# Chunk 1's three rounds u = v + N u in a DeltaNet + SwiGLU kernel: units of odd bp on exchanged halves

## The chip, the cores and the metric

One core of one Trainium2 chip runs the whole program in one launch. The metric is device time in microseconds. Three runs of the kernel before gave 695.55, 698.75 and 694.11 us; their median is 695.55. Everything is float32.

## The reference

Two blocks, one after the other. The first is a gated delta rule: for each of 4 batches and 8 heads a 48x48 state is read and updated token by token over 768 tokens. Its output is laid side by side by head (8 x 48 = 384 columns) for 3072 tokens and goes through a SwiGLU feed-forward block.

```python
B, H, S, D = 4, 8, 768, 48
k_n = k / (norm(k) + 1e-06)
for t in range(S):
    kt, vt, bt = k_n[:, :, t], v[:, :, t], beta[:, :, t, None]
    y[:, :, t] = einsum('bhd,bhde->bhe', q[:, :, t], state)
    v_old = einsum('bhde,bhd->bhe', state, kt)
    state = state + bt[..., None] * einsum('bhd,bhe->bhde', kt, vt - v_old)
x = y.transpose(0, 2, 1, 3).reshape(3072, 384)
g, val = x @ w_gate, x @ w_val            # 384 x 1536 each
out = (g / (1 + exp(-g)) * val) @ w_out   # 1536 x 384
```

## The kernel before

The 768 tokens are cut into 12 chunks of 64. Inside a chunk the recurrence is a triangular system over 64 tokens, one for each of the 32 pairs of batch and head. A pair is called a unit, and has four indices: b and bp (batch = 2 b + bp), j and par (head = 2 j + par). A unit's 64 tokens lie in one half of the 128 partitions, rows 0 to 63 or 64 to 127; `half_of(x)` is that half. TensorE is used as four quadrants of 64x64: the half that a unit's operands lie in is the quadrant's rows, the half of PSUM's partitions that it writes to is its columns.

For chunks 2 and later the inverse of the triangular matrix is made whole, by VectorE or GpSimd. For chunks 0 and 1, which stand at the head of the program, only the four diagonal blocks of 16 tokens are inverted (`zt`), and the rest is done by rounds. A matrix N is formed for each unit (L734, from `l_sb` and `zt`, copied from PSUM to `n_sb` by ScalarE at L739). Then v0 is the product of `zt` and the scaled v (L950), copied to SBUF at L962, and three times u = v0 + N u is taken: 32 products of a 64x64 N and a 64x48 u on TensorE (L970), then one sum on VectorE over 128x768 (L1353, in the helper `plus`). Four blocks of 16 are why three rounds are enough.

`advance(c)` is a generator that does this for chunk c. For c = 1 it yields after the v0 products and after each of the first two rounds, and the driver puts half of a feed-forward product (L1282: three matmuls of 128x128 by 256) behind each yield, with one or two conversions of weight pieces. So the order of work on each engine is written out in the program; there is no other scheduler. Round, half product, round, half product, round, half product, then the state's update (L1018, added at L1027) and the chunk's output (L1006, copied to `y` at L1063 and L1065), then transposes (L1079, copied at L1085).

In chunk 1 `every()` walks the units in the order bp, j, then (par, b) = (0,0), (1,1), (0,1), (1,0). L950 reads rows of half b ^ par and writes half b; the N products read half b ^ par and write half b too. After that a unit's N, v0 and u all lie in half b, and the rounds (`by_par` with flip = 0) read half b and write half b. One bank holds par 0, the other par 1.

At the same time the weights come in. Each is loaded as words in pieces, put together by ScalarE (L272, L278) and VectorE (L289, L297, L309), and each piece's place is loaded again by SyncE when its conversion is done (L260). SyncE also loads q, k and v of later chunks (L140, L186). ScalarE makes silu (L1291), VectorE the product with the second factor (L1293). L1309 is the output product of the first two chunks; from chunk 2 on the feed-forward block takes other forms (L1186, L1392).

Of the kernel before, what the change touches and what calls it, by code (L numbers as in the profile page):

```python
# [8 lines left out]
FP32 = mybir.dt.float32  # L9
# [4 lines left out]
C = 64  # L14
# [6 lines left out]
def kernel(  # L21
# [25 lines left out]
    nc = tc.nc  # L47

    B, H, S, D = q.shape
    NCH = S // C  # L50
    NJ = H // 2
    NB = B // 2
# [5 lines left out]
    HH = NB * H  # L58
# [4 lines left out]
    work = ctx.enter_context(tc.tile_pool(name="work", bufs=2))  # L63
# [10 lines left out]
    def ps_pair(name, tag):  # L74

        return pairs_of_banks[tag]
# [21 lines left out]
    qpad = [const.tile([128, NB, H, DP], FP32, name=f"qpad{i}") for i in range(QB)]  # L98
# [224 lines left out]
    for b in range(2):  # L323
        rows = mask_q[64 * b : 64 * b + 64]
        nc.gpsimd.affine_select(
            out=rows,
            in_=rows,
# [23 lines left out]
    def half_of(x):  # L351
        return slice(64 * x, 64 * x + 64)
# [4 lines left out]
    def every():  # L357
        for bp in range(NB):
            for j in range(NJ):
                for n, (par, b) in enumerate(ORDER):  # L360
                    yield bp, j, par, b, bp == 0 and j == 0
# [104 lines left out]
    def scale_v(c, engine=nc.vector):  # L466
        scaled.add(c)
        if c > 1:
            spent.append(1.4)
        r = vin[c].rearrange("p par bp j d -> p (par bp j) d")  # L470
        n = n_t[c // 2][:, c % 2, :, None].to_broadcast([128, HH, D])
        engine.tensor_tensor(out=r, in0=r, in1=n, op=ALU.mult)

    def banks(name, tag):

        if type(tag) is int:
            return [ps_ffn([128, 512], name, tag + i) for i in range(2)]
        p = ps_pair(name, tag)
        return [p[:, 0], p[:, 1]]
# [87 lines left out]
    WAIT, MORE = "wait", "more"  # L567
# [40 lines left out]
    first_of, l_sb, n_sb = {}, {}, {}  # L608
# [118 lines left out]
    def n_products(c, p_n, pars):  # L727

        zt = ztp[0][:, c]
        p_v = [p.rearrange("p (bp j i) -> p bp j i", bp=NB, j=NJ) for p in p_n]  # L730
        for bp, j, par, b, _ in every():
            if par in pars:
                rows, h = half_of(b ^ par), HH // 2 * par + NJ * bp + j
                nc.tensor.matmul(  # L734
                    p_v[par][half_of(b), bp, j], l_sb[c][rows, h], zt[rows, h]
                )

    def n_copy(c, p_n, par):
        nc.scalar.copy(  # L739
            n_sb[c][:, par].rearrange("p bp j i -> p (bp j i)"), p_n[par]  # L740
        )

    def new_nt(c, flat):
        n_sb[c] = flat.rearrange("p (par bp j i) -> p par bp j i", bp=NB, par=2, j=NJ)

    def recur(p, m=D):
        p = p[:, :, 0 : NB * NJ * m]
        return p.rearrange("p x (bp j d) -> p x bp j d", bp=NB, j=NJ)
# [150 lines left out]
    def advance(c):  # L899

        kn = kn_of(c)
        zt = ztp[c // 2 % ZB][:, c % 2]
        zt = zt.rearrange("p (par bp j) i -> p par bp j i", par=2, bp=NB)
# [3 lines left out]
        if c > 0:  # L907
            p_y = recur(ps_pair("p_y", "py"))
            p_r = recur(ps_pair("p_r", "px"))
            for bp, j, par, b, first in every():  # L910
# [4 lines left out]
                    start=first,  # L915
                    stop=True,
                    skip_group_check=True,
                )
            for bp, j, par, b, first in every():
# [4 lines left out]
                    start=first,  # L924
                    stop=False,
                    skip_group_check=True,
# [4 lines left out]
        def new_u(name):  # L931
            return work.tile([128, 2, NB, NJ, D], FP32, name=name, tag="r", bufs=2)

        def single(bank):
            return [
                p[:, 0 : NB * NJ * D].rearrange("p (bp j d) -> p bp j d", bp=NB, j=NJ)
                for p in banks("p_u", bank)
            ]

        p_u = recur(ps_pair("p_u", "px"))  # L940
        p_u_of = [p_u[:, 0], p_u[:, 1]]

        v0 = new_u("uu" if c > 1 else "v0")
        if c == 0:
            p_n = banks("p_n", "py")
            n_products(c, p_n, (0, 1))
            for par in range(2):
                n_copy(c, p_n, par)
        for bp, j, par, b, first in every():
            nc.tensor.matmul(  # L950
                p_u_of[par][half_of(b), bp, j],
                zt[half_of(b ^ par), par, bp, j],
                r[half_of(b ^ par), par, bp, j],
                start=first,
                stop=True,
                skip_group_check=True,
            )
        if c == 0:
            nc.vector.tensor_copy(v0[:, 0], p_u[:, 0])
            nc.scalar.copy(v0[:, 1], p_u[:, 1])  # L960
        else:
            nc.scalar.copy(v0, p_u)  # L962
        uu = v0

        def by_par(p, stationary, moving, flip, start):
            for par in range(2):
                for bp in range(NB):
                    for j in range(NJ):
                        for b in range(2):
                            nc.tensor.matmul(  # L970
                                p[par][half_of(b ^ par * flip), bp, j],
                                stationary[half_of(b), par, bp, j],
                                moving[half_of(b), par, bp, j],
                                start=start and bp + j == 0,
                                stop=True,
                                skip_group_check=True,
                            )
                yield par

        if c < 2:  # L980
            yield MORE
            uu = new_u("uu")
            p_n = single(2) if c == 0 else p_u_of
            for n in range(3):
                for par in by_par(p_n, n_sb[c], uu if n else v0, 0, True):
                    if c == 0:
                        plus(uu[:, par], v0[:, par], p_n[par])
                        if n + par < 3:
                            yield MORE
                if c > 0:  # L990
                    plus(uu, v0, p_u)
                    if n < 2:
                        yield MORE
        if c + 2 < NCH:
            if c < 2:
# [45 lines left out]
        if c == 0:  # L1041
            third = single(2)[0]
            for par in range(2):
                for bp in range(NB):
                    p = third if par and bp else p_y[par]
                    for j in range(NJ):
                        for b in range(2):
# [4 lines left out]
                                start=j == 0 and (bp == 0 or par == 1),  # L1052
                                stop=True,
                                skip_group_check=True,
# [20 lines left out]
        for bp in range(NB):  # L1075
            for t in range(KT):
                at = slice(t * 128, (t + 1) * 128)
                p = p_f[bp][:, t] if c == 0 else p_f[:, t, bp]
# [26 lines left out]
    def units(t):  # L1105
        return t.rearrange("p (u n) -> p u n", u=4)
# [74 lines left out]
    p_x, p_w, p_y, p_v = (units(bank) for bank in ffn_banks)  # L1181
# [170 lines left out]
    def plus(out, a, b):  # L1352
        nc.vector.tensor_tensor(out=out, in0=a, in1=b, op=ALU.add)  # L1353
# [235 lines left out]
    def point(c):  # L1589

        mine = c < NCH and steps("advance", c) < 4 and may_advance(c)
        if mine and steps("advance", c) > 0:
            step("advance", advance, c)
        elif not prep_step(c - 1) and mine:
            step("advance", advance, c)

    def finish(c):

        if c < NCH:
            while not may_advance(c):  # L1600
                fill_some(1000)
                prep_step(c - 1)
            while steps("advance", c) < 4:
                step("advance", advance, c)
# [27 lines left out]
    with tc.manual_schedule(  # L1632
# [63 lines left out]
        zb_1 = work.tile([128, R, R], FP32, name="zb", bufs=1)  # L1696
# [11 lines left out]
        converts_first(2)  # L1708
        p_n = banks("p_n", "px")
        n_products(1, p_n, (0,))  # L1710
        step("advance", advance, 0)
        converts_first(4)
        n_products(1, p_n, (1,))
        converts_first(1, 3)
        converts_first(5)
        scale_v(1)
        for par in range(2):
            n_copy(1, p_n, par)

        def chain(at):  # L1720

# [70 lines left out]
```

## Time and profile before

| | |
|---|---|
| median of three runs | 695.55 us (694.11 to 698.75) |
| the profiled execution | 697.58 us, of which the span from first to last instruction is 695.9 us |
| instructions | 25446 |
| mean granted TensorE clock | 0.996 of full |
| TensorE busy, 46.0 to 58.1 us | 10.63 of 12.10 us |
| TensorE busy, 75.2 to 140 us | 64.75 of 64.80 us |
| HBM | 53.58 MB read, 7.08 MB written |

The profile is of one execution. Times in it are counted from the start of its span. PE is TensorE's matmuls, PEld its weight loads (which overlap), DVE is VectorE, ACT ScalarE, POOL GpSimd, SP SyncE. In a timeline a row has the start, the length from the first start to the last end, engine, line, operation, what it writes and reads, partitions and elements, and how many records it merges; a bracket at the end is the idle time of the engine before it and what ended it. A 64x64 or 128x128 float32 matmul is two matmul records and two weight loads. The length of a TensorE row has the last matmul's latency in it, so that the next row starts before it is over: the time that a row takes is read from start to start. "issue" is a wait for nothing that the profile shows.

### The profile page before, as it was taken

Reading aid. Unit: us, or ns where it says so; the run is one execution under the profiler, and the core shown is the slowest. Engines: PE = TensorE matmul, PEld = TensorE weight load, DVE = VectorE, ACT = ScalarE, POOL = GpSimd, SP = SyncE. Lnnn points to the kernel's source line nnn. Section 1 sums busy time; section 2 is a strip of 40 time slices with the busy share of each in tenths; the row PEclk is TensorE's granted clock in tenths of the full one; section 3 lists DMA queues with packets and bytes.
Section 4 is the critical chain, followed back from the end, with each engine's and each line's share of the span. In section 5 each row is a group of like instructions: output and inputs, shape, how many; then the busy total and the mean of one; then the engine's idle time right before and its main releaser. Section 6 shows DMA issues by size and latency. Waiting matters only on the chain.

```text
span 695.9 us, 25446 instructions
## 1 busy us (share of the span) xinstructions
PE 680.5 (98%) x11272; PEld 634.9 (91%) x11272; DVE 410.3 (59%) x857; ACT 258.7 (37%) x548; POOL 192.3 (28%) x310
## 2 busy tenths in 40 slices
PE   7799999999999999999999999999999999999997
PEld 4597888756999999999999999999999999999997
DVE  6876789798666745557446547465565345333342
ACT  4754776204543533343333245233143242142230
POOL 5010031105893037830037830328800000000000
PEclk9999999999999999999999999999999999999999
DMA  9566925006561532464333373233263221221210
GB/s 133 141 167 171 288 63 167 1 23 156 140 121 25 103 92 40 92 118 92 78 86 70 67 138 73 56 83 73 64 122 70 55 63 46 56 62 46 69 47 23
DMA packets 143854, 62.29 MB, mean 90 GB/s; under 512 B 122977, under 2 KB 126049, under 8 KB 143745
## 3 DMA queue, kind: packets, MB, share of 16 engines
q1 hardware_dynamic: 141536, 60.19, 37.5%
q8 instruction: 88, 1.44, 0.9%
q10 hardware_dynamic: 2080, 0.39, 0.4%
q14 instruction: 22, 0.17, 0.1%
q0 software_dynamic: 128, 0.10, 0.1%
HBM read 53.58 MB, written 7.08 MB: 87 GB/s over the span
## 4 chain that ended last, share of the span: by engine, by line
PE 93%; SPq 2%; DMA 2%; ACT 1%; issue 1%; DVE 1%; POOL 0%; DVEq 0%; ACTq 0%
PE ffn L1186 43%; PE ffn L1392 20%; PE ffn L1282 9%; PE ffn L1309 4%; PE p_px L950 2%; PE p_px L911 2%; PE p_py L920 2%; PE p_px L1018 1%; PE p_py L1006 1%; PE p_py L521 1%; SPq L140 1%; PE p_px L521 1%; PE ffn L970 1%; DMA h_f<-in_moe_w_gate_dram 1%; PE p_py L1079 1%
## 5 line engine op out<-in xcount | busy, mean ns | idle before, releaser
L1186 PE MATMUL ffn<-x_ffn,wg_sb 128*128 128x128 f32 x840 | 128.2, 275 | 0.0
L1186 PE MATMUL ffn<-x_ffn,wv_sb 128*128 128x128 f32 x840 | 128.1, 275 | 0.0
L1186 PEld LDWEIGHTS ffn<-x_ffn,wg_sb 128*128 128x128 f32 x840 | 111.1, 192 | 0.1
L1186 PEld LDWEIGHTS ffn<-x_ffn,wv_sb 128*128 128x128 f32 x840 | 110.7, 192 | 0.0
L1221 DVE TENSOR_TENSOR h_f<-sil,ffn 128x256 f32<-128x256 f32 x120 | 50.0, 418 | 78.5 <-ACT sil L1216 76.9
L1216 ACT ACTIVATE sil<-ffn 128x256 f32<-128x256 f32 x120 | 46.0, 383 | 132.6 <-PE ffn L1186 130.9
L1392 PE MATMUL ffn<-wo_sb,h_f 128*128 128x192 f32 x480 | 83.4, 327 | 0.0
L813 POOL TENSOR_TENSOR n_b<-mb,half 128x32 f32<-128x32 f32 x5 | 30.0, 6008 | 182.2 <-DVE mb L563 182.2
L1392 PEld LDWEIGHTS ffn<-wo_sb,h_f 128*128 128x128 f32 x480 | 78.1, 190 | 0.4
L1353 DVE TENSOR_TENSOR ffn<-ffn,p_sb 128x512 f32<-128x512 f32 x58 | 40.5, 699 | 63.7 <-ACT ffn L1242 62.4
L599 POOL TENSOR_TENSOR zb<-zb,tmp 128x31 f32<-128x31 f32 (+15 forms) x124 | 71.5, 576 | 9.7
L593 POOL TENSOR_TENSOR tmp<-zb,mb 128x31 f32<-128x31 f32 (+15 forms) x124 | 67.0, 541 | 16.0 <-DVE mb L580 6.6
L1186 PE MATMUL ffn<-x_t,h_f 128*128 128x128 f32 x480 | 61.1, 280 | 0.2 <-ACT ffn L1199 0.2
L1186 PEld LDWEIGHTS ffn<-x_t,h_f 128*128 128x128 f32 x480 | 56.2, 191 | 1.4 <-ACT ffn L1199 0.4
L1353 DVE TENSOR_TENSOR o_sb<-o_sb,ffn 128x192 f32<-128x192 f32 x49 | 17.2, 352 | 61.9 <-PE ffn L1392 60.7
L1199 ACT COPY ffn<-ffn 128x512 f32<-128x512 f32 x30 | 17.1, 571 | 63.9 <-PE ffn L1186 57.5
L1392 PE MATMUL ffn<-last_k,h_f 128*128 128x192 f32 x200 | 35.9, 327 | 0.0
L1350 DVE TENSOR_TENSOR h_f<-h_f,h_f 128x256 f32<-128x256 f32 x60 | 30.2, 512 | 9.2 <-PE ffn L1392 8.2
L1282 PE MATMUL ffn<-x_ffn,wg_sb 128*128 128x256 f32 x144 | 34.3, 384 | 0.0
L1282 PE MATMUL ffn<-x_ffn,wv_sb 128*128 128x256 f32 x144 | 33.8, 382 | 0.0
L1392 PEld LDWEIGHTS ffn<-last_k,h_f 128*128 128x128 f32 x200 | 32.9, 190 | 0.0
L1282 PEld LDWEIGHTS ffn<-x_ffn,wv_sb 128*128 128x128 f32 x144 | 27.0, 190 | 3.7
(300 smaller groups left out, 1095.6 us busy)
## 6 DMA issues: line engine op xcount, KB each, us to landing
h_f<-w_s SPq DMA_DIRECT2D x60, 256.0 KB, 2.9
p_sb<-w_s SPq DMA_DIRECT2D x27, 256.0 KB, 2.8
vin<-in_v_dram SPq DMA_DIRECT2D x48, 96.0 KB, 3.4
out_dram<-o_sb SPq DMA_DIRECT2D x48, 96.0 KB, 2.2
kn<-in_k_dram SPq DMA_DIRECT2D x20, 192.0 KB, 4.6
zt<-in_moe_w_out_dram SPq DMA_DIRECT2D x6, 384.0 KB, 3.3
qpad<-in_q_dram SPq DMA_DIRECT2D x36, 64.0 KB, 3.1
w_s<-h_f SPq DMA_DIRECT2D x7, 256.0 KB, 4.2
```

The lines of the kernel that those rows point to most:

```text
L593: engine.tensor_tensor(out=t_v, in0=zb[:, 0 : j + 1, j : j + 1].to_broadcast([128, j + 1, m]), in1=mb[:, j : j + 1, j + 1 : R].to_broadcas ...
L599: engine.tensor_tensor(out=zb[:, 0 : j + 1, j + 1 : R], in0=zb[:, 0 : j + 1, j + 1 : R], in1=t_v, op=ALU.add,)
L813: nc.gpsimd.tensor_tensor(out=n, in0=mb.rearrange("p j i -> p (j i)")[:, 0 : R * R : R + 1], in1=half, op=ALU.pow,)
L1186: nc.tensor.matmul(p[:, u], w(u), moving, start=start and u == 0, stop=True, skip_group_check=True,)
L1199: nc.scalar.copy(p_y, p_x)
L1216: nc.scalar.activation(sil[:, n].rearrange("p (i n) -> p i n", i=2), p[:, 0:2], ACTF.Silu)
L1221: nc.vector.tensor_tensor(out=h_of(c, f, j), in0=sil[:, n].rearrange("p (i n) -> p i n", i=2), in1=p[:, 2:4], op=ALU.mult,)
L1282: nc.tensor.matmul(ps[name][:, i], w_sb[:, t, (f + i) * 128 : (f + i + 1) * 128], xts[c][:, t], start=(t == 0 and i == 0), stop=(t == KT - 1),
L1309: nc.tensor.matmul(p_o, hs[c, f - f % 2][:, f % 2, bp * 128 : (bp + 1) * 128], wo_sb[:, f], start=(f == 0), stop=(f == FT - 1),)
L1350: nc.vector.tensor_tensor(out=out, in0=a, in1=b, op=ALU.subtract)
L1353: nc.vector.tensor_tensor(out=out, in0=a, in1=b, op=ALU.add)
L1392: nc.tensor.matmul(p[x, part], a(f - f % 2)[:, f % 2], b(f), start=not begun and f == 0, stop=f == FH - 1, skip_group_check=True,)
```

## The change

The change is in chunk 1 alone, and in its rounds. Units with bp = 1 change halves before each round and come back in the next, so that of four units one after the other (bp = 0 and 1, b = 0 and 1) each uses another quadrant.

- The N products write a unit with bp = 1 to the other half, and into bank par ^ bp. ScalarE copies them by bank to the places they had (`by_bank`), and makes a second copy of the N of bp = 1 with its halves exchanged again (`n_turned`, two copies of 64x512).
- The v0 products do likewise. ScalarE copies them by bank to v0 (two copies of 128x384), and makes v1, which is v0 with bp = 1 exchanged (two copies of 64x384, and one of 128x384 for bp = 0). v1 lies in `qpad[1]`, where chunk 0's N was.
- Rounds 0 and 2 read bp = 1 from half b ^ 1 and write half b; round 1 reads half b, with `n_turned`, and writes half b ^ 1. In each round bank bp holds the units of bp. The sums add v1, v0 and v1 in turn, over four runs of 192 elements.

The number of matmuls and of VectorE's instructions is as before; ScalarE has six copies more. The order of all other instructions on the five queues is the same.

```diff
@@ -731,14 +731,38 @@
         for bp, j, par, b, _ in every():
             if par in pars:
                 rows, h = half_of(b ^ par), HH // 2 * par + NJ * bp + j
-                nc.tensor.matmul(
-                    p_v[par][half_of(b), bp, j], l_sb[c][rows, h], zt[rows, h]
-                )
+                if c == 0:
+                    out = p_v[par][half_of(b), bp, j]
+                else:
+                    out = p_v[par ^ bp][half_of(b ^ bp), par, j]
+                nc.tensor.matmul(out, l_sb[c][rows, h], zt[rows, h])
 
     def n_copy(c, p_n, par):
         nc.scalar.copy(
             n_sb[c][:, par].rearrange("p bp j i -> p (bp j i)"), p_n[par]
         )
+
+    def by_bank(flat, bank):
+
+        x = flat.rearrange("p (x n) -> p x n", x=4)
+        return x[:, 1:3] if bank else x[:, 0:4:3]
+
+    def other_half(flat):
+        return flat.rearrange("p (x n) -> p x n", x=4)[:, 1:4:2]
+
+    def crossed_copies(out, in_):
+        for b in range(2):
+            nc.scalar.copy(out[half_of(b)], in_[half_of(1 - b)])
+
+    def n_copies_1(p_n, flat):
+
+        for bank in range(2):
+            nc.scalar.copy(
+                by_bank(flat, bank), p_n[bank].rearrange("p (x n) -> p x n", x=2)
+            )
+        n_turned = work.tile([128, 2, NJ * C], FP32, name="n_turned", tag="z1", bufs=1)
+        crossed_copies(n_turned, other_half(flat))
+        n_sb["turned"] = n_turned.rearrange("p par (j i) -> p par j i", i=C)
 
     def new_nt(c, flat):
         n_sb[c] = flat.rearrange("p (par bp j i) -> p par bp j i", bp=NB, par=2, j=NJ)
@@ -947,8 +971,12 @@
             for par in range(2):
                 n_copy(c, p_n, par)
         for bp, j, par, b, first in every():
+            if c == 1:
+                out = p_u_of[par ^ bp][half_of(b ^ bp), par, j]
+            else:
+                out = p_u_of[par][half_of(b), bp, j]
             nc.tensor.matmul(
-                p_u_of[par][half_of(b), bp, j],
+                out,
                 zt[half_of(b ^ par), par, bp, j],
                 r[half_of(b ^ par), par, bp, j],
                 start=first,
@@ -958,6 +986,15 @@
         if c == 0:
             nc.vector.tensor_copy(v0[:, 0], p_u[:, 0])
             nc.scalar.copy(v0[:, 1], p_u[:, 1])
+        elif c == 1:
+            flat = v0.rearrange("p par bp j d -> p (par bp j d)")
+            for bank in range(2):
+                p = p_u_of[bank].rearrange("p par j d -> p par (j d)")
+                nc.scalar.copy(by_bank(flat, bank), p)
+            v_flat = qpad[1].rearrange("p bp h d -> p (bp h d)")[:, 0 : HH * D]
+            v1 = v_flat.rearrange("p (par bp j d) -> p par bp j d", par=2, bp=NB, j=NJ)
+            crossed_copies(other_half(v_flat), other_half(flat))
+            nc.scalar.copy(v1[:, :, 0], v0[:, :, 0])
         else:
             nc.scalar.copy(v0, p_u)
         uu = v0
@@ -982,14 +1019,37 @@
             uu = new_u("uu")
             p_n = single(2) if c == 0 else p_u_of
             for n in range(3):
+                if c > 0:
+                    u = uu if n else v0
+                    for par in range(2):
+                        for j in range(NJ):
+                            for bp in range(NB):
+                                for b in range(2):
+                                    rows = half_of(b ^ bp ^ (bp * n % 2))
+                                    w = n_sb[c][rows, par, bp, j]
+                                    if bp * n % 2:
+                                        w = n_sb["turned"][rows, par, j]
+                                    nc.tensor.matmul(
+                                        p_u_of[bp][half_of(b ^ (bp * n % 2)), par, j],
+                                        w,
+                                        u[rows, par, bp, j],
+                                        start=par + j == 0,
+                                        stop=True,
+                                        skip_group_check=True,
+                                    )
+                    plus(
+                        uu.rearrange("p par bp j d -> p bp par (j d)"),
+                        (v0 if n % 2 else v1).rearrange(
+                            "p par bp j d -> p bp par (j d)"
+                        ),
+                        p_u.rearrange("p bp par j d -> p bp par (j d)"),
+                    )
+                    if n < 2:
+                        yield MORE
+                    continue
                 for par in by_par(p_n, n_sb[c], uu if n else v0, 0, True):
-                    if c == 0:
-                        plus(uu[:, par], v0[:, par], p_n[par])
-                        if n + par < 3:
-                            yield MORE
-                if c > 0:
-                    plus(uu, v0, p_u)
-                    if n < 2:
+                    plus(uu[:, par], v0[:, par], p_n[par])
+                    if n + par < 3:
                         yield MORE
         if c + 2 < NCH:
             if c < 2:
@@ -1714,8 +1774,7 @@
         converts_first(1, 3)
         converts_first(5)
         scale_v(1)
-        for par in range(2):
-            n_copy(1, p_n, par)
+        n_copies_1(p_n, zb_1.rearrange("p k i -> p (k i)"))
 
         def chain(at):
```

## The prediction

> **What bounds the kernel now.** I read the page first, then busy times by stretch, then the order of work on TensorE around chunk 1's rounds, and last the queues of VectorE and ScalarE beside them. The page's busy shares:
>
> ```profile
> PE 680.5 (98%) x11272; PEld 634.9 (91%) x11272; DVE 410.3 (59%) x857; ACT 258.7 (37%) x548; POOL 192.3 (28%) x310
> ...
> q8 instruction: 88, 1.44, 0.9%
> ```
>
> TensorE (PE) is the bound. The q8 line is for later: 1.44 MB in 88 transfers, against 11272 weight loads and 11272 matmuls, is one transfer for every 256 of PE's instructions. By stretch (PE busy first; the clock, DMA share and GB/s at the end):
>
> ```profile
> 58.10:68.60 10.50, 10.50 (x211) 9.00 (x210) 6.69 (x15) 4.34 (x12) 0.48 (x3) 1.00 0.78 193
> ...
> 140.00:400.00 260.00, 259.20 (x4871) 242.63 (x4870) 163.83 (x311) 91.54 (x192) 121.32 (x181) 1.00 0.40 87
> 400.00:690.00 290.00, 290.00 (x4236) 286.02 (x4235) 138.35 (x278) 88.11 (x189) 46.15 (x79) 1.00 0.29 67
> ```
>
> PE is full while chunk 1's rounds run (58.1 to 68.6) and, but for 0.8 us, from 140 to 690. So PE time removed from the rounds reaches the end, if PE finds no wait between 60 and 140. The timeline of PE there (start, length, engine, line, what, records; one matmul of the code is two records):
>
> ```profile
> 53.75 0.43 PE L920 MATMUL p_py<-state,qt 48*64 48x48 f32 x10 [1.47 <-issue]
> 54.11 1.56 PE L1282 MATMUL ffn<-x_ffn,wv_sb 128*128 128x256 f32 x6
> 55.60 1.15 PE L950 MATMUL p_px<-vin,zt 64*64 64x48 f32 x64
> 56.68 1.56 PE L1282 MATMUL ffn<-x_ffn,wv_sb 128*128 128x256 f32 x6
> ...
> 61.66 2.07 PE L970 MATMUL p_px<-uu,zb 64*64 64x48 f32 x64
> 63.66 1.56 PE L1282 MATMUL ffn<-x_ffn,wg_sb 128*128 128x256 f32 x6
> 65.15 2.07 PE L970 MATMUL p_px<-uu,zb 64*64 64x48 f32 x64
> 67.15 1.56 PE L1282 MATMUL ffn<-x_ffn,wv_sb 128*128 128x256 f32 x6
> 68.64 0.94 PE L1018 MATMUL p_px<-uu,kn 64*48 64x48 f32 x64
> 69.40 1.11 PE L1006 MATMUL p_py<-uu,p_sb 64*64 64x48 f32 x64
> 70.44 1.56 PE L1282 MATMUL ffn<-x_ffn,wv_sb 128*128 128x256 f32 x6
> ```
>
> Go by starts: a round of 32 units takes 61.66 to 63.66 = 2.00 us; L950, also 32 units of 64x64 by 48, takes 55.60 to 56.68 = 1.08; L1006 takes 1.04. The difference is the quadrants: by the code a round multiplies rows of half b into columns of half b alone (two of four), L950 and L1006 use all four. Between rounds lie three feed-forward matmuls (six records, 1.49 us), which cover VectorE's sum.
>
> **The change, part by part.** *Rounds.* Each block of four units now names four different quadrants, in round 0 and 2 in the order of rows 0, 1, 1, 0 and columns 0, 1, 0, 1, as L1018 has it. Same units, same 64-column weights. Price by L950 and L1006: 1.04 to 1.08, so 0.92 to 0.96 saved a round; three rounds, 2.8 us. L1018's 0.76 is for 48-column weights, and would be 3.7 us: the outer end.
>
> A row of this trace tells whether two row halves may fill one bank together: L950 puts rows of both halves into each of its two banks and still takes 1.08, so I keep the 2.8. The Trainium skill speaks against it (TensorEngine Tiling (Array Packing), Gotcha 1: PSUM Pressure): different row tiles cannot use one PSUM bank at the same time. By that rule the new rounds, which put both row halves into each bank, would stay at 2.00 us and the sum would lose the whole 2.8; L950's row disagrees with it.
>
> *Solve (L950) and N products (L734).* Outputs change place only; each call covers the same quadrants as often. Nothing.
>
> *VectorE's sums.* The same 768 elements, read by bank. Its queue:
>
> ```profile
> 60.35 0.95 DVE L1353 TENSOR_TENSOR uu<-v,p_px 128x768 f32<-128x768 f32 x1 [1.32 <-PE p_px L970]
> ...
> 63.77 0.95 DVE L1353 TENSOR_TENSOR uu<-v,p_px 128x768 f32<-128x768 f32 x1 [1.34 <-PE p_px L970]
> ...
> 67.27 0.95 DVE L1353 TENSOR_TENSOR uu<-v,p_px 128x768 f32<-128x768 f32 x1 [0.79 <-PE p_px L970]
> ```
>
> It idled 1.32, 1.34 and 0.79 us before them; between them lie weight conversions of 1.21 us (after the first) and 1.83 us (after the second). With rounds of 1.05 a sum comes every 2.54 us. The first gap holds 0.88 + 1.21, the second 0.88 + 1.83 = 2.71: the third sum starts 0.17 late. A sum starts 0.11 after its round and ends 0.43 before the 1.49 us of cover does, so 0.17 costs nothing; beyond 0.43 every microsecond counts.
>
> *ScalarE's copies.* Before N's use: two crossed copies of 64x512 more. After the solve: one copy of 128x768 becomes two of half the size, two crossed of 64x384 and one of 128x384. The neighbours:
>
> ```profile
> 46.37 1.07 ACT L739 COPY zb<-p_px 128x512 f32<-128x512 f32 x2 [0.94 <-PE p_px L734]
> 48.97 0.80 ACT L1030 COPY state<-p_px 128x768 f32<-128x768 f32 x1 [1.52 <-PE p_px L1018]
> ```
>
> Crossed 64x512: between 0.54 each (L739) and 0.98 each (L809's copies of 32x1024 in SBUF, 3.93 us for two, 1.92 ns an element). So 1.1 to 2.0 us into an idle of 1.52: at worst L1030 is 0.45 late, and PE reads state at 50.32, 0.55 after L1030 ended. Nothing. After the solve: the rows of 384 elements take 0.48 (L1063, L1065), five of them 2.4 us for 0.80; at L809's rate 2.9. Round 0 needs the first two, 56.81 + 0.96 = 57.8, and starts at 58.17: nothing. The first sum needs the last, 59.2 (at worst 59.7); round 0 now ends at 59.2, so at worst the sum is 0.4 late, inside its 0.43. Behind these copies on ScalarE stand weight conversions, 1.6 us late. VectorE uses them late: what it takes at 61.23 ScalarE wrote at 51.68. Nothing, with some 8 us of cover.
>
> *Feeding PE.* At 53.75 PE has waited 1.47 us on nothing but "issue", in the middle of dense 64x48 work. The packets of q8 in the trace start at 51.15, 54.96, 61.05, 67.01 and 70.43; PE went on 2.60 after 51.15. Counting 128 weight loads from that stall, blocks end at 59.39 (in round 0), 66.02 (in round 2) and 69.70 (in L1006), where the last transfer lay 4.4, 5.0 and 2.7 us back: enough. Denser rounds bring the ends to 58.9, 63.8 and 67.2. With transfers starting 1.66 and 0.99 after the ends before (the lags of 61.05 and 67.01), they lie 3.2 and 2.4 back: the second is 0.2 short of 2.60. I take 0.2 us, between 0 and one such stall, 1.47. The Trainium skill (Runtime: NRT & Kernel Launch, Instruction fetch mechanics) calls a block's fetch mostly hidden. By it this term is 0 and the sum 2.8; the 1.47 us disagrees.
>
> *What is late next.* Moving PE 2.6 us forward from 69 on, I look for what can't follow. ScalarE waited 1.94 us for a weight transfer until 81.65 and then runs nearly without a gap to 97; VectorE's product at 97.52 to 98.20 hangs on it, and its bank is written again at 101.06. If that transfer lands no earlier, 2.9 us of cover meet a shift of 2.6: nothing. SyncE issues back to back there, but on conversions that move forward, so it lands somewhat earlier. The order of SyncE's and GpSimd's queues doesn't change.
>
> Sum: −2.8 + 0.2 = −2.6 us. The profiled execution took 697.58 (span 695.9, 1.7 around it): 695.0. It lies 2.0 above the median of the three, 695.55; from that, **693.0 us**.
>
> **Rivals.** *A, no packing.* The row halves exclude each other in a bank, and rounds stay at 2.00. For it: nothing in this trace, but the exact order of round 1 (rows 0, 1, 0, 1; columns 0, 1, 1, 0) has no row of its own. Against: L950, L1006, L1018. Time: 695.55. Chance 0.06.
>
> *B, the feed takes over, slower.* Place: the block ends at 63.8 and 67.2. Price: 1.47 each, 2.9; and after the idle around 33 the clock stood at 0.66 of full from 35 to 40, a loss of 1.7 us. If that follows too, −2.8 + 2.9 + 1.7 = +1.8: 697.4. It decides from the point where a transfer starts less than 1.1 us before a block's end (2.60 less 1.47), by either slower starts or DMA traffic (share 0.78 here). For: the 1.47 us itself. Against: 1.49 us of sparse feed-forward matmuls stand after each round. Chance 0.06.
>
> *C, half of it is lost before 140.* The transfer at 81.65 and ScalarE's run behind it don't move, and some product or conversion has less cover than the one I followed. Price up to 1.5 us: 694.3. For: ScalarE without a gap, DMA busy. Against: 2.9 us of cover at the place found. Chance 0.10.
>
> **How the numbers follow.** Forecast 0.76, A 0.06, B 0.06, C 0.10; 0.02 for the unforeseen. The forecast's own terms span −2.9 (no issue wait) to −1.3 (a whole one), 692.7 to 694.3. Three runs of one kernel spread from 694.11 to 698.75, so a median may move by 2 us: 690.6 to 696.4, which takes in A and C and leaves out B. One per cent, 7 us, is about what a measurement here can tell from no change. All cases lie within it: rounds of no length at all would give 6.0. Same 0.93; faster 0.03 and slower 0.04 for drift and for B at more than two places.
>
> **What would show it.** Right: three rounds at 1.04 to 1.08 start to start, the groups between them still 1.49 without idle, the third sum with no idle before it, the crossed copies at 0.48 to 0.98 with PE unmoved, at most a short issue wait in L1006, and L1309 beginning 2.6 us before 131.71. Wrong: rounds near 2.0 (A); issue waits over 1 us in round 2 or L1006, or a clock below 1 after 60 (B); PE idle on ScalarE, VectorE or a bank between 75 and 140 (C).

## The result, and the profile after

The changed kernel takes 693.82 us (median of 22 runs, 691.82 to 697.0), the kernel before 695.81 in the same comparison: a ratio of 0.9972, with a 95% interval of 0.9959 to 0.9985. That is 2.0 us less. A second comparison (the last run below) gave 0.9966, 0.9944 to 0.9988.

TensorE around the rounds, in the timeline of the changed kernel (L978 is the solve that was L950, L1032 the rounds, L1342 the feed-forward group, L1078 and L1066 the state's update and the output; of the second round only the first row stands here, because its rows change stationary operand every other unit):

```profile
52.60 1.15 PE L978 MATMUL p_px<-vin,zt 64*64 64x48 f32 x64
53.68 1.56 PE L1342 MATMUL ffn<-x_ffn,wv_sb 128*128 128x256 f32 x6
55.17 1.15 PE L1032 MATMUL p_px<-v,zb 64*64 64x48 f32 x64
56.25 1.56 PE L1342 MATMUL ffn<-x_ffn,wg_sb 128*128 128x256 f32 x6
57.74 0.26 PE L1032 MATMUL p_px<-uu,zb 64*64 64x48 f32 x2
...
58.82 1.56 PE L1342 MATMUL ffn<-x_ffn,wg_sb 128*128 128x256 f32 x6
60.31 1.15 PE L1032 MATMUL p_px<-uu,zb 64*64 64x48 f32 x64
61.39 1.56 PE L1342 MATMUL ffn<-x_ffn,wv_sb 128*128 128x256 f32 x6
62.88 0.94 PE L1078 MATMUL p_px<-uu,kn 64*48 64x48 f32 x64
63.64 0.52 PE L1066 MATMUL p_py<-uu,p_sb 64*64 64x48 f32 x23
64.74 0.80 PE L1066 MATMUL p_py<-uu,p_sb 64*64 64x48 f32 x41 [0.58 <-issue]
65.47 1.56 PE L1342 MATMUL ffn<-x_ffn,wv_sb 128*128 128x256 f32 x6
```

From start to start, a round takes 55.17 to 56.25 = 1.08 us, exactly what L978 takes (52.60 to 53.68), and the groups still take 1.49. The one new thing is the bracket in L1066: 23 records in, TensorE waits for "issue", and the block takes 63.64 to 65.47 = 1.83 us instead of 1.04.

| from start to start, us | before | after |
|---|---|---|
| three rounds | 2.00 each | 1.08 each |
| three groups between them | 1.49 each | 1.49 each |
| first round to the end of the output products | 12.27 | 10.30 |
| from there to the output products of the feed-forward block (L1309) | 61.27 | 61.28 |
| from there to the last matmul's start | 559.75 | 559.84 |

L1309's first row before, and the same product in the changed kernel:

```profile
131.71 22.09 PE L1309 MATMUL ffn<-wo_sb,h_f 128*128 128x384 f32 x68
...
126.75 22.09 PE L1369 MATMUL ffn<-wo_sb,h_f 128*128 128x384 f32 x68
```

The rounds give 3 x 0.92 = 2.76 us, the wait takes 0.79 back, and the remaining 1.97 us reach the end to a tenth of a microsecond. The median moved by 1.99. That the two agree so closely is partly luck: the interval of the ratio allows 1.0 to 2.9 us, and in a second profile of the changed kernel (the last run below) the stretch from the first round to the end of the output products takes 9.77 us, 2.50 less than before.

The span of the profile fell further, from 695.9 to 691.0. The other 3.0 us lie before the first round (58.17 against 55.17), 2.4 of them between chunk 0's first round and its state's update: in the profile of before the clock stood at half for 3.41 us there, while in that of the changed kernel it stayed full, and a wait for "issue" took 1.33 us, not 0.56. Two profiles of variants of the changed kernel (the fourth and the fifth below) have that dip too, so it is no effect of the change. Two single spans can't be compared here; stretches from one instruction to another can. The stretch from 35 to 40 us, before and then changed (PE busy first; the clock, the DMA share and GB/s at the end):

```profile
35.00:40.00 5.00, 5.00 (x126) 5.00 (x123) 1.92 (x4) 4.10 (x13) 0.55 (x3) 0.66 0.39 113
...
35.00:40.00 5.00, 5.00 (x181) 5.00 (x179) 3.47 (x8) 3.55 (x12) 0.43 (x3) 1.00 0.52 154
```

VectorE's sums and ScalarE's copies in the changed kernel:

```profile
56.45 0.95 DVE L1413 TENSOR_TENSOR uu<-qpad,p_px 128x768 f32<-128x768 f32 x1 [0.42 <-PE p_px L1032]
...
58.95 0.95 DVE L1413 TENSOR_TENSOR uu<-v,p_px 128x768 f32<-128x768 f32 x1 [0.42 <-PE p_px L1032]
...
61.57 0.95 DVE L1413 TENSOR_TENSOR uu<-qpad,p_px 128x768 f32<-128x768 f32 x1
```

```profile
44.38 1.25 ACT L755 COPY n_turned<-zb 64x512 f32<-64x512 f32 x2
46.01 0.80 ACT L1090 COPY state<-p_px 128x768 f32<-128x768 f32 x1 [0.39 <-PE p_px L1078]
...
53.82 0.86 ACT L993 COPY v<-p_px 128x384 f32<-128x384 f32 x2 [0.95 <-PE p_px L978]
54.71 1.03 ACT L755 COPY qpad<-v 64x384 f32<-64x384 f32 x2
55.75 0.51 ACT L997 COPY qpad<-v 128x384 f32<-128x384 f32 x1
```

A sum by bank takes 0.95 us as before. VectorE still idles before the first two, and takes the third with no idle, 0.18 us after the round's end; it ends at 62.52, before the group does at 62.88. On ScalarE the copies of v take 53.82 to 56.26, and L1090 behind the copies of N still waits for TensorE.

### The profile page after: what moved, and what is told of

It is laid out like the page before. It is cut to its first block, busy times and chain, and to the rows that moved or that the text cites. A ratio compares the mean times of both kernels' runs of the same rounds, so it can differ in the third digit from the quotient of the medians.

```text
span 691.0 us, 25452 instructions
## 1 busy us (share of the span) xinstructions
PE 676.8 (98%) x11272; PEld 630.7 (91%) x11272; DVE 410.0 (59%) x857; ACT 261.9 (38%) x554; POOL 192.9 (28%) x310
## 4 chain that ended last, share of the span: by engine, by line
PE 93%; DMA 2%; SPq 2%; ACT 1%; DVE 1%; issue 1%; POOL 0%; DVEq 0%; ACTq 0%
PE ffn L1246 44%; PE ffn L1452 20%; PE ffn L1342 9%; PE ffn L1369 4%; PE p_px L978 2%; PE p_px L935 2%; PE p_py L944 2%; PE p_px L1078 1%; PE p_py L1066 1%; PE p_py L521 1%; SPq L140 1%; PE p_px L521 1%; DMA h_f<-in_moe_w_gate_dram 1%; PE p_py L1139 1%; PE ffn L1007 1%
## 5 line engine op out<-in xcount | busy, mean ns | idle before, releaser
L1342 PE MATMUL ffn<-x_ffn,wg_sb 128*128 128x256 f32 x144 | 34.3, 385 | 0.0
L1342 PE MATMUL ffn<-x_ffn,wv_sb 128*128 128x256 f32 x144 | 33.8, 382 | 0.0
L1342 PEld LDWEIGHTS ffn<-x_ffn,wv_sb 128*128 128x128 f32 x144 | 27.0, 190 | 3.7
```

The costliest lines, as they stand in the source:

```text
L1342: nc.tensor.matmul(ps[name][:, i], w_sb[:, t, (f + i) * 128 : (f + i + 1) * 128], xts[c][:, t], start=(t == 0 and i == 0), stop=(t == KT - 1),
```

## The experiments

The theory: the gain is the packing of four quadrants, 2.76 us, and what is lost again is lost to instruction supply, which comes in blocks of 256 (a transfer of q8 each) and is too slow where dense blocks of products stand close. The rivals: something else in the change shortens or lengthens the stretch (banks, copies), or the waits for "issue" belong to the products they stand in.

**Two quadrants at a time, all else as changed.**

```diff
-                    for par in range(2):
-                        for j in range(NJ):
-                            for bp in range(NB):
+                    for bp in range(NB):
+                        for par in range(2):
+                            for j in range(NJ):
```

> The changed kernel with one difference: in each round all units of bp = 0 come first and then all of bp = 1, so that only two quadrants are in use at a time; ScalarE's six additional copies, the halves and the banks stay. Theory (the saving is the packing of four quadrants, and the copies cost nothing): each round goes back from 1.08 to 2.0 us from start to start, 2.8 us in all, the issue wait in L1066's place disappears as the stream is sparser again, and the time is that of the kernel before (ratio 0.999 to 1.001). Rival (the banks or the copies by bank shorten something else): rounds or the path between them stay shorter and the ratio stays near 0.997. Second rival (the copies do cost): rounds at 2.0 and over 0.5 us of new waits of TensorE between the rounds, ratio above 1.001.

Measured: ratio 0.9985 (0.9965 to 1.0004). Timeline of TensorE:

```profile
63.08 1.88 PE L1032 MATMUL p_px<-uu,zb 64*64 64x48 f32 x64
64.89 1.56 PE L1342 MATMUL ffn<-x_ffn,wv_sb 128*128 128x256 f32 x6
...
67.87 0.80 PE L1066 MATMUL p_py<-uu,p_sb 64*64 64x48 f32 x41 [0.21 <-issue]
```

A round takes 63.08 to 64.89 = 1.81 us: 0.73 of the 0.92 is gone by the order alone, with copies, halves and banks kept. The groups stay at 1.49, so the copies cost TensorE nothing. The order also changes how the two banks take turns: in this run bank 0 is filled before bank 1, as in the kernel before. No run here separates that from the quadrants for 64x64 products. But the trace of before has two groups of 128 records of 32x32 products, each in four parts of the array; L874 writes one bank, L888 two in turn:

```profile
241.50 1.29 PE L874 MATMUL p_px<-zt,a_sb 32*32 32x32 f32 x128
242.72 0.49 PE L1186 MATMUL ffn<-x_t,h_f 128*128 128x128 f32 x2
...
247.38 1.29 PE L888 MATMUL p_py<-t,z 32*32 32x32 f32 x128
248.59 0.60 PE L1186 MATMUL ffn<-x_ffn,p_sb 128*128 128x128 f32 x3
```

From start to start they take 1.22 and 1.21 us, which speaks against the banks.

The interval of the ratio holds 1, as the theory has it, and also the rival's 0.997 near its edge, so the total doesn't decide; the rounds do. Two details were not expected: 1.81 instead of 2.00 (see the last section), and the wait in the output products shrank (0.42 us by starts, not 0.79) and did not vanish.

**The stream moved by 68 pairs.** A pair is a weight load and a matmul; `unread_small` is `unread` with 32x16 instead of 32x512.

```diff
-        unread(3)
+        unread(2)
+        unread_small(35)
```

> The changed kernel; at the head one of three filler matmuls of 32x512 (results unread) is replaced by 35 small ones of 32x16, so that all later TensorE instructions stand 68 pairs of weight load and matmul later in the stream; nothing that is computed changes. Theory (the issue waits come where one 256-instruction block is used up before the next has come, so they are bound to a count and not to a place in the program): the 1.40 us wait in the state products of chunk 1 and the 0.58 us wait in the output products of chunk 1 both go; the block ends fall in the second round, in the state's update and 44 pairs into the v0 products, where at most one wait of 0.4 to 1.4 us appears; from the start of chunk 1's state products to the end of its output products 0.6 to 1.6 us are saved. Rival (the waits belong to those products themselves, or to a buffer): they stay at 1.4 and 0.6 us in the same lines.

Measured: ratio 1.0006 (0.9985 to 1.0026). Lines are 6 higher than in the changed kernel (L950 the q products, L984 the v0 products, L1072 the output):

```profile
51.45 1.11 PE L950 MATMUL p_py<-state,qt 48*64 48x48 f32 x64
...
53.99 0.90 PE L984 MATMUL p_px<-vin,zt 64*64 64x48 f32 x43
55.49 0.56 PE L984 MATMUL p_px<-vin,zt 64*64 64x48 f32 x21 [0.60 <-issue]
...
65.94 1.11 PE L1072 MATMUL p_py<-uu,p_sb 64*64 64x48 f32 x64
...
71.07 1.06 PE L505 MATMUL p_px<-ident,kn 128*128 128x128 f32 x8 [1.52 <-DMA kn<-in_k_dram]
```

Both waits are gone from the q products and the output products, and one stands 43 records into the v0 products, where it was expected. From the first state products to the end of the output products it takes 16.49 us against 18.08: 1.59 less. The rival falls: a wait moves with the count of instructions before it. The total did not gain, since all later block ends moved too: from L1309's place to the last matmul this profile takes 563.8 us, 4.0 more than the changed kernel's, with new waits for "issue" there, of which 1.06 us at 168.7 and 0.77 at 345.9 are the longest. And TensorE, ahead of its loads by now, waited 1.52 us for k of a later chunk. A place found for one dense stretch is no place for the others.

**The stream moved by 94 pairs** (`unread_small(48)`).

> As the run with 35 small filler matmuls, but with 48 of them: 94 pairs more than in the changed kernel. Theory (count): block ends fall at the end of the third round and 58 pairs into the output products, with one feed-forward group between them; an issue wait of 0.8 to 1.5 us stands about 58 pairs into the output products, longer than the 0.58 us of the changed kernel, and none stands where that one was (24 pairs into them); the 1.40 us wait in the second state products goes. Rival: waits as in the changed kernel.

One run took 695.37 us (the kernel before has a median of 697.45 in the same comparison); a single total decides nothing here. Timeline of TensorE:

```profile
64.92 1.03 PE L1072 MATMUL p_py<-uu,p_sb 64*64 64x48 f32 x57
66.39 0.33 PE L1072 MATMUL p_py<-uu,p_sb 64*64 64x48 f32 x7 [0.45 <-issue]
```

With 94 pairs more, a block end lies 94 pairs earlier and the next one 128 later: 24 − 94 + 128 = 58 pairs into the output products, and there, after 57 records, the wait stands. After 23 nothing is left, and the q products run without a wait. Its size was missed: 0.70 us by starts (0.45 in the bracket), not 0.8 to 1.5.

**v1 made twice.**

```diff
+            for _ in range(2):
                 crossed_copies(other_half(v_flat), other_half(flat))
                 nc.scalar.copy(v1[:, :, 0], v0[:, :, 0])
```

> The changed kernel with the three copies that make v1 made twice, the same values to the same place: some 1.5 us more on ScalarE before the first sum. Theory (the copies are free because the first sum may end 0.4 us late under the feed-forward group, and conversions behind them have 8 us of cover): v1 is done at about 1.4 us after the first round's end, the sum ends about 1.0 us after the group, and TensorE waits 1.0 us for VectorE before the second round, nothing elsewhere. Rival A (there is more cover than that): no wait. Rival B (conversions behind the copies are needed at once): further waits of TensorE on VectorE or ScalarE in the feed-forward groups up to 75 us.

One run took 696.72 us, beside the same 697.45. From the list of waits (total, times, longest), and then from the timeline:

```profile
PE p_px L1033 <- DVE uu L1414: 1.1, 1, 1.1
...
58.54 1.56 PE L1343 MATMUL ffn<-x_ffn,wg_sb 128*128 128x256 f32 x6
61.23 0.26 PE L1033 MATMUL p_px<-uu,zb 64*64 64x48 f32 x2 [1.13 <-DVE uu L1414]
```

TensorE waits once, 1.13 us before the second round, and in no feed-forward group up to 75 us for VectorE or ScalarE. Some 1.5 us more of copies cost 1.2 by starts (58.54 to 61.23 is 2.69, instead of 1.49). So the cover over the copies is a few tenths of a microsecond, as the 0.43 of the prediction has it, and the conversions behind them have more: 1.2 us of delay made TensorE wait nowhere else there.

**One group between the dense blocks.** In chunk 1 the q products move behind the feed-forward group that followed them; nothing is added.

```diff
+            if c > 1:
+                of_q()
             nc.vector.tensor_tensor(out=r, in0=r, in1=p_r, op=ALU.subtract)
             yield
+            if c == 1:
+                of_q()
```

> The changed kernel with one group of three feed-forward matmuls moved: in chunk 1 the state products of q come after the group that stood behind them, so that no two dense blocks of 64 pairs stand side by side there; nothing is added or left out. Theory (a block of 256 instructions is used up too fast where dense blocks touch): the issue wait of 1.2 to 1.4 us in the q products goes; the next block end falls 42 pairs into the first round, 3.6 us after the one before, where 0 to 0.6 us of wait may appear; the wait of 0.6 to 0.8 us in the output products stays, since nothing changes between the two block ends before it. From the start of the first state products to the end of the output products 17.0 us plus or minus 0.4 instead of 18.1; against the kernel before a ratio of 0.995 to 0.997, if the changed kernel on the same chip has 0.997 to 0.998. Rival (the wait is the q products' own, such as a wait for their operand or their bank): it stays where they are, and the time is that of the changed kernel.

```profile
52.79 1.15 PE L946 MATMUL p_py<-state,qt 48*64 48x48 f32 x64
53.76 1.11 PE L985 MATMUL p_px<-vin,zt 64*64 64x48 f32 x64
...
57.30 0.56 PE L1039 MATMUL p_px<-v,zb 64*64 64x48 f32 x23 [0.17 <-issue]
...
66.41 0.80 PE L1073 MATMUL p_py<-uu,p_sb 64*64 64x48 f32 x41 [0.70 <-issue]
```

The q products run through, 0.17 us of wait (0.42 by starts) appear 41 records into the first round, and the wait in the output products stays: as expected. The stretch takes 16.92 us, inside what was expected. Against before the ratio is 0.9975 (0.9959 to 0.9991), not the 0.995 to 0.997 that was expected, beside 0.9966 for the changed kernel in the same comparison: the 0.7 to 1.2 us that the stretch lost against the two profiles of the changed kernel are below what these totals can tell, and it is not shown to beat that kernel.

**The changed kernel again.**

> The changed kernel as it is, beside the others on this chip. Theory: ratio 0.997 plus or minus 0.0015; rounds of 1.08 us; issue waits of 1.2 to 1.5 us in the q products and 0.5 to 0.8 us in the output products; from the start of the first state products to the end of the output products 18.1 us plus or minus 0.4. Rival (the issue waits are chance): other lengths or places.

Ratio 0.9966 (0.9944 to 0.9988). List of waits:

```profile
PE p_py L944 <- issue: 1.7, 2, 1.5
```

Timeline of TensorE:

```profile
65.02 1.38 PE L1066 MATMUL p_py<-uu,p_sb 64*64 64x48 f32 x64
66.33 1.56 PE L1342 MATMUL ffn<-x_ffn,wv_sb 128*128 128x256 f32 x6
```

Rounds at 1.08 again, and the wait in the q products at 1.5. In the output products only 0.26 us by starts are lost this time (1.30 instead of 1.04), and the list has no row for it, so its size was expected too high: the place repeats (0.79, 0.92, 0.92 and 0.26 us in the four profiles with that order of rounds and that count), the length does not. The stretch takes 17.65 us, just short of the 17.7 to 18.5 that was expected.

## Why the prediction was right, and where it was off

The forecast was 693.0 us, 2.6 saved, and 693.82 came, 2.0 saved, inside the range. The gain and its cause were as forecast; one term of the sum was too small.

*Rounds.* 2.8 us by L950's and L1006's rows; 2.76 measured, and the run with two quadrants at a time shows that the order of units makes it.

*Rival A, no packing,* falls. Each bank of the new rounds takes rows of both halves, and a round has L978's 1.08 us. The Trainium skill's rule (TensorEngine Tiling (Array Packing), Gotcha 1: PSUM Pressure), by which different row tiles can't use one bank at a time, would have kept 2.00 us; the measurement disagrees, for tiles that write different partitions of the bank.

*Feeding PE* is the term that was mis-sized: "I take 0.2 us, between 0 and one such stall, 1.47". It cost 0.79 in the profile, and 0.26 to 0.92 over four. The place was right, 23 records into L1066 for the 24th that was counted, and the mechanism held when the stream was moved by 68 and by 94 pairs. What failed is above all the lag, taken from single rows. A block's transfer starts some time after the block before is used up: 0.99 us was the row used for this place, 1.74 was measured (60.72, the last weight load of the block before, to 62.46, the packet of q8). By the prediction's own sum the wait is that lag less 0.8 (63.8 + lag + 2.60 − 67.2), so 0.9 for the lag measured. Two more terms were off, and nearly cancel: TensorE went on 2.28 us after the transfer's start, not 2.60, and the block lasted 3.19 us (60.72 to 63.91), not 3.4. The 67.2 behind that 3.4 was worked out wrong: three rounds shorter by 0.92 each take 69.70 to 66.9. In the last run the lag was 0.99 and 0.26 us were lost, where the sum gives 0.2, but again with 2.50 and 3.18 for the other two. The trace of before had lags of 0.7 to 2.9 at the ends of its blocks between 30 and 71 us. So one row could not give the size, and it was the width of the range, which allowed for a whole stall, that took in the result.

The Trainium skill (Runtime: NRT & Kernel Launch, Instruction fetch mechanics) calls the cost of crossing from block to block mostly hidden. That doesn't hold here, where 128 pairs are used up in 3.2 us and 0.26 to 0.92 us are lost.

*Rival B* was half right: one of its two waits came, at half its price, and the clock stayed at 1.0 after it, up to the last matmul. *Rival C* falls: the stretch from the end of the output products to L1309 is 61.27 before and 61.28 after, so nothing was lost under the weight conversions. The run moved by 68 pairs shows what would have come next: k of a later chunk, where TensorE waited 1.52 us. That load was not among those that the prediction followed under what is late next. The forecast's sign, L1309 2.6 us before 131.71, can't be read from the spans: it came at 126.75, 4.96 earlier, of which 3.0 lie before the rounds and 1.97 behind their start.

*Copies and sums at nothing* held. The crossed copies took 0.62 us (64x512) and 0.52 (64x384), in the bounds of 0.54 to 0.98 and 0.48 to 0.74; the third sum started without idle as worked out. The run with v1 twice shows that the cover over the copies of v1 is thin.

## What to carry to other kernels

Here four products in four quadrants cost what two in two do, so the units of a batch are worth spreading over exchanged halves if an idle engine can make the crossed copies. Price a denser instruction stream by how long 256 instructions last: between 30 and 70 us waits came where they lasted 3.0 to 3.5 us, and not every time (a block of 3.42 us in the run moved by 94 pairs went without). Where single runs spread by more than the gain, compare stretches from one instruction to another, not spans.

## What the runs showed of the hardware

In the rounds with two quadrants, TensorE takes one matmul record in each of the two in a step of 58 ns; 64 records are 32 steps, 1.86 us, and 0.14 of ends. With four quadrants the step is still 58 ns and takes four records: 16 steps. In the run with all of bp = 0 first, the steps around the change from one pair of quadrants to the other, some six units, held records of both pairs, and about three steps were saved: 1.81 us instead of 2.00. In its second round the first matmul of bp = 1 starts at 60.52, the last of bp = 0 at 60.69. So matmuls of other quadrants begin beside earlier ones some units ahead, without being written next to them; that this is why was only read from the starts.

The waits for "issue" follow TensorE's own count of 256 instructions. Count the matmul records from the start of the program: between 30 and 70 us every wait for "issue" of over 0.15 us, in all eight profiles, stands at the same place of 128, after 87 to 89 records, whatever product is there. After a transfer of q8 starts, TensorE goes on 2.3 to 3.3 us later where it had run out; for block ends between 30 and 65 us the start itself follows the end by 0.6 to 3.0 us, and for those just behind by up to 7.3. What sets that lag stays open.
